# Retention and routed experts: decays as full products, tables built on the chip, loads ahead of row sends, and the first expert's weights by quarters

## The chip, the cores and the metric

The kernel runs on one core of one Trainium2 chip. The metric is the device time of one execution in microseconds (us); lower is better. Names of engines: PE is TensorE, DVE is VectorE, ACT is ScalarE, POOL is GpSimd, SP is SyncE, which here only issues DMA transfers. SPq and POOLq are the queues of instructions that SP and POOL issue.

## The reference

Retention over 4 batches, 8 heads, 768 steps and 64 values per head gives 3072 tokens of 512 values. These are routed greedily, by the highest logits first, to 8 experts with room for 384 tokens each, and every expert is two matrix products with a ReLU between them.

```python
gamma = 1.0 - 2.0 ** (-5.0 - np.arange(H, dtype=np.float32))
scale = 1.0 / np.sqrt(D)
for t in range(S):
    state = gamma[None, :, None, None] * state + np.einsum('bhd,bhe->bhde', k[:, :, t], v[:, :, t])
    y[:, :, t] = scale * np.einsum('bhd,bhde->bhe', q[:, :, t], state)
...
logits = x @ w_gate
order = np.argsort(-logits.flatten())
for idx in order:
    tok, e = (int(idx) // E, int(idx) % E)
    if assigned[tok] >= 0 or counts[e] >= cap:
        continue
    assigned[tok] = e
    counts[e] += 1
...
for e in range(E):
    mask = assigned == e
    h = np.maximum(x[mask] @ w1[e], 0.0)
    out[mask] = h @ w2[e]
```

## The kernel before

**Retention.** The 768 steps are cut into 6 chunks of 128, so there are 24 units (batch, chunk), chunk by chunk: unit 0 to 3 are chunk 0 of the four batches. Each unit comes in one load (`ld`) of 1 MB: keys and queries by columns, values and keys by rows (0.75 MB in the last chunk, which needs no state). There are 8 buffers for loads (DEEP), so the load of unit u + 8 needs the buffer of unit u. Units 0 to 3 are worked one at a time, the others two at a time (a group). Per unit PE does the scores (`scores`, 8 matmuls with 64 rows, recorded as 16), for chunks after the first the old state's part of the output (`outputs`), the mix of scores and values (`mix`) and the state's update (`states`). In between DVE multiplies the scores with the decay table `dm` into `am`, POOL scales keys (`ks`) and queries (`qs`), and ACT copies outputs (`ys`) and states (`T`).

**Start.** The decay table `dm` is made by `decays`: 8 matmuls of two tables with a single row each, times the triangle `upper`. PE runs matmuls on a tile of zeros (`warm`, function `busy`, counts in WARM) before the decays, before and after the scores of unit 0. The table `qtab` scales queries from chunk 1 on, `ktab` keys, `cst` and `thr` serve routing, `ident` is the unit matrix for transposes. All come by loads on SP, between the units' loads. SP's order is decided by the scheduler, PE's is that of the code, and within retention DVE's and ACT's also.

**Rows and routing.** Finished outputs become rows of tokens: 17 units by DVE transposes that SP sends to `xs` in memory (`block_rows`, `send_long`, `send_one`, 36 sends), seven by PE transposes (`early_rows`, `rows_out`), an ACT copy `xr` and a send. The logits go into a search over thresholds on DVE and PE (`search`): compare tokens with thresholds (`cmp`), count pairs by a matmul of `cmp` and the one-hot `oh` (`by_two`), and from the counts the threshold (`th`, `q`, `nmb` and others). Its result, the token list `idx`, lets POOL gather the expert's tokens (`xg`) and weights (`wraw`).

**Experts.** Each float32 operand is split into a high and a low part: `w1h` on ACT and `w1l` on DVE, `xh` and `xlo` the same after a turn of the gathered tokens on PE (`turn_x`, tile `pt`, two buffers). mm1 has for each of 8 blocks f twelve products of 128x384 (`ph`), mm2 24 products of 128x512 for each of 3 tiles of tokens (`py`). For expert 0 the first high products are done as thirds of 128 tokens as they arrive (`by_thirds`), after a fill of idle PE (HOT matmuls); mm1 then does the rest of these blocks. The search for the next expert (`side`) runs beside mm1 and mm2. A planner with estimated times (`clk`) sets the order of code; `side.held` stops the search from being stepped while an `xlo` is pending.

## Time and profile before

| | us |
|---|---|
| median of 3 runs (413.46 to 415.4) | 413.63 |
| profiled execution, own time | 416.51 |
| its span, first to last instruction | 414.7 |
| PE busy | 394.7 (95%) |
| DVE, ACT, POOL busy | 272.1, 157.5, 141.7 |
| mean granted clock of PE | 0.991 |

The own time of the profiled execution is 1.8 us more than its span, and 2.9 us more than the median of the runs. Of the span, retention takes about the first 91 us, routing and the start of the first expert's work the time to 117 us, and the eight experts the rest.

### The profile page before, as it was taken

Reading aid. Unit: us, or ns where it says so; the run is one execution under the profiler, and the core shown is the slowest. Engines: PE = TensorE matmul, PEld = TensorE weight load, DVE = VectorE, ACT = ScalarE, POOL = GpSimd, SP = SyncE. Lnnn points to the kernel's source line nnn. Section 1 sums busy time; section 2 is a strip of 40 time slices with the busy share of each in tenths; the row PEclk is TensorE's granted clock in tenths of the full one; section 3 lists DMA queues with packets and bytes.
Section 4 is the critical chain, followed back from the end, with each engine's and each line's share of the span. In section 5 each row is a group of like instructions: output and inputs, shape, how many; then the busy total and the mean of one; then the engine's idle time right before and its main releaser. Section 6 shows DMA issues by size and latency. Waiting matters only on the chain.

```text
span 414.7 us, 8494 instructions
## 1 busy us (share of the span) xinstructions
PE 394.7 (95%) x3464; PEld 343.8 (83%) x3465; DVE 272.1 (66%) x637; ACT 157.5 (38%) x287; POOL 141.7 (34%) x158
## 2 busy tenths in 40 slices
PE   8999988997899999998999999998999999999994
PEld 7888987986499779886887897897789889989983
DVE  1438768796989758766977795779488457246400
ACT  1342332423346056133525343543344347156210
POOL 2369873300520440074044251134125217120011
PEclk9999999998999999998999999999999999999999
DMA  7999997937673291339329447047325714901001
GB/s 239 415 417 420 398 307 255 268 83 235 194 286 106 60 320 77 103 109 338 112 55 322 145 140 305 25 149 258 129 66 173 293 51 119 387 28 51 2 27 57
DMA packets 23538, 77.99 MB, mean 188 GB/s; under 512 B 2626, under 2 KB 11970, under 8 KB 17092
## 3 DMA queue, kind: packets, MB, share of 16 engines
q0 software_dynamic: 8592, 46.14, 32.1%
q1 hardware_dynamic: 14900, 31.23, 21.1%
q8 instruction: 29, 0.48, 0.5%
q14 instruction: 17, 0.14, 0.1%
HBM read 64.78 MB, written 12.58 MB: 187 GB/s over the span
## 4 chain that ended last, share of the span: by engine, by line
PE 60%; issue 14%; DVE 11%; DMA 9%; POOL 2%; ACT 2%; SPq 0%; POOLq 0%; DVEq 0%
PE py L1038 23%; PE ph L1016 22%; DMA ld<-qkv 9%; PE yp L388 3%; PE sc L343 2%; PE pt L966 2%; PE psm L146 2%; DVE w2l L146 1%; POOL out L1046 1%; PE yp L373 1%; PE TP L407 1%; DVE cmp L146 1%; POOL wraw L914 1%; PE sc L473 1%; PE ph L995 1%
## 5 line engine op out<-in xcount | busy, mean ns | idle before, releaser
L1016 PE MATMUL ph<-xh,w1h 128*128 128x384 f32 x244 | 81.4, 348 | 2.5 <-ACT xh L971 1.5
L1016 PE MATMUL ph<-xh,w1l 128*128 128x384 f32 x256 | 81.7, 338 | 0.0
L1016 PE MATMUL ph<-xlo,w1h 128*128 128x384 f32 x256 | 81.3, 336 | 0.0
L1038 PE MATMUL py<-w2h,hh 128*128 128x512 f32 x192 | 78.1, 407 | 0.0
L1038 PE MATMUL py<-w2l,hh 128*128 128x512 f32 x192 | 75.2, 392 | 1.0 <-DVE w2l L146 1.0
L1038 PE MATMUL py<-w2h,hl 128*128 128x512 f32 x192 | 75.1, 391 | 0.0
L1046 POOL DMA_INDIRECT out<-yo,oix x24 | 26.1, 1086 | 104.4 <-ACT yo L1044 85.2
L1021 ACT ACTIVATE hh<-ph 128x384 fp32r<-128x384 f32 x64 | 31.5, 491 | 64.2 <-PE ph L1016 61.3
L146 DVE SCALAR_TENSOR_TENSOR hl<-ph,hh 128x384 fp32r<-128x384 f32 x64 | 34.6, 553 | 25.7 <-ACT hh L1021 25.3
L914 POOL DMA_INDIRECT wraw<-w,wix x31 | 33.9, 1093 | 47.4 <-DVE un L146 34.3
L1016 PEld LDWEIGHTS ph<-xh,w1h 128*128 128x128 f32 x244 | 45.9, 190 | 4.0 <-ACT xh L971 1.9
L146 DVE TENSOR_TENSOR w1l<-wraw,w1h 128x1024 fp32r<-128x1024 f32 (+1 forms) x36 | 39.3, 1102 | 14.4 <-ACT w1h L932 14.2
L1016 PEld LDWEIGHTS ph<-xh,w1l 128*128 128x128 f32 x256 | 48.2, 190 | 0.0
L953 POOL DMA_INDIRECT xg<-xs,idx x24 | 30.9, 1288 | 49.6 <-issue 33.5
L1016 PEld LDWEIGHTS ph<-xlo,w1h 128*128 128x128 f32 x256 | 47.8, 189 | 0.0
L346 DVE TENSOR_TENSOR am<-sc,dm 128x512 f32<-128x512 f32 x48 | 30.1, 683 | 25.0 <-PE sc L343 25.0
L1038 PEld LDWEIGHTS py<-w2l,hh 128*128 128x128 f32 x192 | 36.2, 188 | 8.2 <-DVE w2l L146 2.2
L1038 PEld LDWEIGHTS py<-w2h,hl 128*128 128x128 f32 x192 | 36.0, 188 | 7.7
L1038 PEld LDWEIGHTS py<-w2h,hh 128*128 128x128 f32 x192 | 36.1, 188 | 5.9
L1044 ACT ACTIVATE yo<-py 128x512 f32<-128x512 f32 x24 | 14.4, 599 | 67.3 <-PE py L1038 37.1
L146 DVE TENSOR_TENSOR w2l<-wraw,w2h 128x1024 fp32r<-128x1024 f32 x32 | 38.5, 1218 | 1.4 <-ACT w2h L932 1.4
L932 ACT ACTIVATE w1h<-wraw 128x1024 fp32r<-128x1024 f32 (+1 forms) x36 | 33.8, 957 | 7.3 <-DMA wraw<-w,wix 7.2
(169 smaller groups left out, 548.3 us busy)
## 6 DMA issues: line engine op xcount, KB each, us to landing
ld<-qkv SPq DMA_DIRECT2D x19, 1024.0 KB, 13.2
xs<-x SPq DMA_DIRECT2D x16, 192.0 KB, 5.2
ld<-qkv SPq DMA_DIRECT2D x4, 768.0 KB, 6.2
xs<-xr SPq DMA_DIRECT2D x7, 256.0 KB, 2.1
xs<-x SPq DMA_DIRECT2D x20, 64.0 KB, 1.8
ld<-qkv SPq DMA_DIRECT2D x2, 512.0 KB, 5.6
wraw<-w,wix POOLq DMA_INDIRECT x33, 7.3
xg<-xs,idx POOLq DMA_INDIRECT x24, 3.8
```

Source lines behind the costliest of these rows:

```text
L146: return f(o, *a, **k)
L343: nc.tensor.matmul(sc[s][:, pr, :], k_[r, w], q_[r, w], start=True, stop=True)
L346: nc.vector.tensor_tensor(am[:, s], sc[s], dm[:, s], op=OP.mult)
L388: nc.tensor.matmul(yp[o:o + 64, pr, :], values(u)[:, 2 * pr + s, :], st[u][0][:, s, pr, :], start=(not c and pr == 0), stop=(pr == HP - 1) ...
L914: nc.gpsimd.indirect_dma_start(out=t, out_offset=None, in_=w1v if nm == "w1" else w2v, in_offset=bass.IndirectOffsetOnAxis(ap=wix[:, hf:hf ...
L932: nc.scalar.activation(p[0], p[2], AF.Copy)
L953: nc.gpsimd.indirect_dma_start(out=t, out_offset=None, in_=xs, in_offset=bass.IndirectOffsetOnAxis(ap=found[n][0][:, j:j + 1], axis=0))
L1016: nc.tensor.matmul(ph, a[:, o:o + 128], x_[:, d], start=(k == 0 and not begun), stop=(k == len(prods) - 1), skip_group_check=begun)
L1021: nc.scalar.activation(hh[:, f], ph, AF.Relu)
L1038: nc.tensor.matmul(py, h_[:, f, t], a[:, o:o + DM], start=(k == 0), stop=(k == 23))
L1044: nc.scalar.activation(yo, py, AF.Copy)
L1046: sct = nc.gpsimd.indirect_dma_start(out=out, out_offset=bass.IndirectOffsetOnAxis(ap=oix[:, j:j + 1], axis=0), in_=yo, in_offset=None, bo ...
```

## The change

The decay table is made from products of 128 rows: the two single rows are copied into tiles that are zero elsewhere. The triangle `upper`, `ident`, the triangle `ub` and the counting row `iot` are built by POOL; `qtab` is made by one matmul of 2 rows and an ACT copy (`q_decay`); `cst` shrinks from 229 to 37 columns, and `thr` is loaded after the last unit. Unit 0 comes in one transfer in place of two. SP follows the order of the code, which places every send of rows behind the last load. Within a group, each unit's states follow its own mix. The last row transposes are spread differently (early_rows three in place of two, by one each). The second 512 KB quarter of w1 is fetched behind the three gathers of x, and its high and low parts are made after the thirds; the thirds cover blocks 0 and 1 in place of 0, 1 and 2. The search's steps are held for experts 0 and 1 while an `xlo` is pending, before only for expert 0. Numbers of warming and filling matmuls change with it.

```diff
-WARM = (10, 4, 6)
+WARM = (12, 6, 6)
...
 SEND = 10, 12
-EARLY = 2
-COLD = 2
-HOT = 22
-THIRDS = 3
+COLD = 4
+HOT = 18
+THIRDS = 2
 FILL = (4, 7)
...
     def consts_on_chip():
-        for t, name in ((ub, "tri"), (codet, "code"), (codeo, "code"), (tokc, "tokc")):
+        for t, name in ((codet, "code"), (codeo, "code"), (tokc, "tokc")):
             nc.scalar.activation(t, c_(name), AF.Copy)
 
     def constants():
         for t, x in [(onesb, 1.0), (un, 1.0)] + [(t, 0.0) for t in (zer512, Sc, Wq, bad, *sgs)]:
             nc.gpsimd.memset(t, x)
+        nc.gpsimd.affine_select(ub, onesb, pattern=[[1, 128]], compare_op=OP.is_gt, fill=0.0, base=0,
+                                channel_multiplier=-1)
+        nc.gpsimd.affine_select(ident, onesb, pattern=[[1, 128]], compare_op=OP.is_equal, fill=0.0, base=0,
+                                channel_multiplier=-1)
+        nc.gpsimd.iota(iot, pattern=[[1, 64]], base=0, channel_multiplier=0, allow_small_or_imprecise_dtypes=True)
 
...
     nc.vector.memset(warm, 0.0)
-    dec = [rw.tile([1, H, C], F32, name="am", bufs=4) for _ in range(2)]
+    dec = [rw.tile([128, 2, HP, C], F32, name="am", bufs=4) for _ in range(2)]
+    rowd = [rw.tile([1, 2, HP, C], F32, name="am", bufs=4) for _ in range(2)]
+    qsel = rc.tile([2, 128], F32, name="qsel")
+    qr = rw.tile([2, HP * C], F32, name="qs", bufs=4)
     up = rw.tile([128, HP, C], F32, name="qs", bufs=4)[:, 0]
+    nc.vector.memset(dec[0], 0.0)
+    nc.gpsimd.memset(dec[1], 0.0)
+    nc.gpsimd.memset(up, 1.0)
+    nc.gpsimd.affine_select(up, up, pattern=[[1, C]], compare_op=OP.is_ge, fill=0.0, base=0, channel_multiplier=-1)
 
...
             for i in range(2):
-                nc.sync.dma_start(dec[i], decay[:, i])
-            nc.sync.dma_start(up, upper)
-        ways = ((0, 2), (2, 4)) if u == 0 else ((0, 4),) if c < NC - 1 else ((0, 3),)
-        for w0, w1_ in ways:
-            nc.sync.dma_start(LD[u][:, w0:w1_], qkv[u, :, w0:w1_])
-            if u == 0 and w0 == 0:
-                nc.sync.dma_start(ktb, ktab)
+                nc.sync.dma_start(rowd[i], decay[:, i])
+        w1_ = 4 if c < NC - 1 else 3
+        nc.sync.dma_start(LD[u][:, 0:w1_], qkv[u, :, 0:w1_])
+        if u == 0:
+            nc.sync.dma_start(ktb, ktab)
+            nc.sync.dma_start(qsel, qrow[:, 0:128])
+            nc.sync.dma_start(qr, qrow[:, 128:])
         if u == B:
             nc.sync.dma_start(wgf, wg)
-            nc.sync.dma_start(ident, idm)
-        if u == B - 1:
-            nc.sync.dma_start(qtb, qtab)
-        if u == B + 1:
+        if u == B + 2:
             nc.sync.dma_start(cs, cst)
+        if u == nu - 1:
             nc.sync.dma_start(ti, thr)
 
     def decays():
 
         for s in range(2):
+            for i in range(2):
+                nc.vector.tensor_copy(dec[i][0:1, s], rowd[i][:, s])
+        for s in range(2):
             ps = bank()
             for pr in range(HP):
-                h = 2 * pr + s
-                nc.tensor.matmul(ps[:, pr, :], dec[0][:, h, :], dec[1][:, h, :], start=True, stop=True)
+                nc.tensor.matmul(ps[:, pr, :], dec[0][:, s, pr, :], dec[1][:, s, pr, :], start=True, stop=True)
             nc.vector.tensor_tensor(dm[:, s], ps, up[:, None, :].to_broadcast([128, HP, C]), op=OP.mult)
 
+    def q_decay():
+
+        ps = bank()
+        nc.tensor.matmul(ps.rearrange("p a b -> p (a b)"), qsel, qr, start=True, stop=True)
+        nc.scalar.activation(qtb, ps, AF.Copy)
+
     def bank():
...
     units = [(b, c) for c in range(NC) for b in range(B)]
+    nu = len(units)
+    ctx.enter_context(tc.manual_schedule(engines={nc.tensor.engine, nc.sync.engine}))
     for u in range(DEEP):
...
 
-    ctx.enter_context(tc.manual_schedule(engines={nc.tensor.engine}))
     wp = rp.tile([128, 512], F32, name="sc", bufs=4)
     busy(WARM[0], wp[:, 0:256])
     m0, a0, oh0, cmp0 = prep_tiles()
     parts, whole, ended, th0 = None, [], None, None
-    nu = len(units)
     groups = [[u] for u in range(B)] + [[u, u + 1] for u in range(B, nu, 2)]
...
             if not g:
+                q_decay()
                 busy(WARM[2], wp[:, 0:256])
...
                 guess()
-            mix(us)
-            states(us)
+            for u in us:
+                mix([u])
+                states([u])
             if g == len(groups) - 2:
...
             send_one(i)
-        early_rows(EARLY // 2)
+        early_rows(1)
         c = NC - 1
         gate(c)
-        early_rows(EARLY // 2)
+        early_rows(1)
         lt = rp.tile([128, 512], F32, name="sc", bufs=4)
         nc.tensor.transpose(lt[:, 0:128], gs[c % 2], ident)
         cols, Lc = slice(c, COLS, NC), lt[:, 0:128].rearrange("p (b x) -> p b x", b=B)[:, :, 0:E]
         f = best(Lc, cols, m0, oh0)
         reach(cols, B, m0, cmp0, th0)
         f()
+        early_rows(1)
         for b in range(B):
...
             raw["w1", 0, 0] = mp.tile([128, 2048], F32, name="wraw", bufs=5)
-            for k in range(2):
-                fetch_first(k, wix4)
+            firsts["w1"] = wix4
+            fetch_first(0, wix4)
         if not last:
...
         fetch_x(0, j)
+    fetch_first(1, firsts.pop("w1"))
     fetch_w("w1", 1, 0, found[0][1])
     for _ in range(4):
         side.step()
     fill(HOT)
     quarters = [parts_w("w1", 0, 0, 512 * q, 512) for q in range(4)]
-    for p in quarters[0:3]:
+    for p in quarters[0:2]:
         high_w(p)
     lows = []
     for j in range(KT):
         turn_x(0, j, lows)
         if not j:
             side.step()
-            high_w(quarters[3])
         else:
             by_thirds(j - 1, range(THIRDS))
-        low_w(quarters[j])
+        if j < KT - 1:
+            low_w(quarters[j])
         lows.pop(0)[1]()
     by_thirds(KT - 1, range(THIRDS))
-    low_w(quarters[3])
+    for p in quarters[2:4]:
+        high_w(p)
+        low_w(p)
     nc.gpsimd.tensor_copy(spacer, xt[0][0][0:1, HP - 1, CAP - 1:CAP].bitcast(F32))
...
     feed = Feed()
-    side.held = lambda: not feed.n and feed.xlows
+    side.held = lambda: feed.n < 2 and feed.xlows
     clk.pe = max(clk.pe, arrive["x", KT - 1, 0] + 2500)
```

SP, the loads of the start, before (`am` holds the decay rows and `qs` the triangle here, `ktb`, `qtb`, `wgf`, `cs`, `ti` are tables):

```order
L306 DMA am<-decay 1x1024 x2
L307 DMA qs<-upper 128x128
L310 DMA ld<-qkv 128x1024
L312 DMA ktb<-ktab 128x72
L310 DMA ld<-qkv 128x1024
L310 DMA ld<-qkv 128x2048 x3
L317 DMA qtb<-qtab 128x512
L310 DMA ld<-qkv 128x2048
L314 DMA wgf<-wg 128x256
L315 DMA ident<-idm 128x128
L310 DMA ld<-qkv 128x2048
L319 DMA cs<-cst 128x229
```

SP, the same place in the change (`qs` now holds the row from which `qtb` is made, `qsel` the two rows that select it):

```order
L317 DMA am<-decay 1x1024 x2
L319 DMA ld<-qkv 128x2048
L321 DMA ktb<-ktab 128x72
L322 DMA qsel<-qrow 2x128
L323 DMA qs<-qrow 2x512
L319 DMA ld<-qkv 128x2048 x4
L325 DMA wgf<-wg 128x256
L319 DMA ld<-qkv 128x2048 x2
L327 DMA cs<-cst 128x37
```

Between the first table and the load of unit 8 stand fewer and smaller tables. SP, the last loads and the first sends of rows, before:

```order
L310 DMA ld<-qkv 128x2048 x14
L450 DMA xs<-x_490 32x12x128
L310 DMA ld<-qkv 128x1536 x2
L450 DMA xs<-x_490 32x12x128 x3
L310 DMA ld<-qkv 128x1536 x2
L450 DMA xs<-x_492 32x12x128 x4
```

and in the change:

```order
L319 DMA ld<-qkv 128x2048 x13
L319 DMA ld<-qkv 128x1536 x4
L329 DMA ti<-thr 128x256
L467 DMA xs<-x_510 32x12x128 x4
L467 DMA xs<-x_512 32x12x128 x4
L467 DMA xs<-x_619 32x12x128 x4
```

One send stood before the load of unit 20 and three before that of unit 22; now all loads and `ti` stand ahead of them.

PE at the first expert, before: the turns of the second and third tile of x (`pt`, `py`), the thirds (128x128) and the beginning of mm1:

```order
L966 MATMUL pt<-ident,xg 128x128 x4
L995 MATMUL ph<-xh,w1h_1784 128x128 x12
L966 MATMUL py<-ident,xg 128x128 x4
L995 MATMUL ph<-xh,w1h_1784 128x128 x24
L1016 MATMUL ph<-xh,w1l_1785 128x384 x4
L1016 MATMUL ph<-xlo,w1h_1784 128x384 x4
L1016 MATMUL ph<-xh,w1l_1785 128x384 x3
```

and in the change:

```order
L986 MATMUL pt<-ident,xg 128x128 x4
L1015 MATMUL ph<-xh,w1h_1800 128x128 x8
L986 MATMUL py<-ident,xg 128x128 x4
L1015 MATMUL ph<-xh,w1h_1800 128x128 x16
L1036 MATMUL ph<-xh,w1l_1801 128x384 x4
L1036 MATMUL ph<-xlo,w1h_1800 128x384 x4
L1036 MATMUL ph<-xh,w1l_1801 128x384 x4
L1036 MATMUL ph<-xlo,w1h_1800 128x384 x4
```

Between the turns stand 8 thirds in place of 12, behind them 16 in place of 24, and the third block of mm1 is no longer begun.

DVE at the turn from expert 1 to expert 2, before: the search's steps (`sg`, `nmb`, `th`, `cmp`, `q`), the low parts of weights (`w1l`) and of x (`xlo`):

```order
L146 TENSOR_TENSOR w1l_2597<-wraw,w1h_2596 128x1024
L146 SCALAR_TENSOR_TENSOR sg_89<-psm,ng 64x8
L146 TENSOR_REDUCE nmb<-psm 128x1
L146 SCALAR_TENSOR_TENSOR th<-nmb,near,off 128x64
L146 TENSOR_TENSOR cmp<-m,th 128x768
L146 TENSOR_TENSOR w1l_2597<-wraw,w1h_2596 128x1024
L146 TENSOR_TENSOR cmp<-m,th 128x768
L146 SCALAR_TENSOR_TENSOR q<-nmb,near,qn 128x1
L146 TENSOR_TENSOR xlo<-pt,xh 128x4x128 x3
L146 TENSOR_TENSOR w1l_2704<-wraw,w1h_2703 128x1024
```

and in the change:

```order
L150 TENSOR_TENSOR w1l_2605<-wraw,w1h_2604 128x1024
L150 SCALAR_TENSOR_TENSOR sg_90<-psm,ng 64x8
L150 TENSOR_TENSOR w1l_2605<-wraw,w1h_2604 128x1024
L150 TENSOR_TENSOR xlo<-pt,xh 128x4x128 x2
L150 TENSOR_REDUCE nmb<-psm 128x1
L150 SCALAR_TENSOR_TENSOR th<-nmb,near,off 128x64
L150 TENSOR_TENSOR cmp<-m,th 128x768
L150 TENSOR_TENSOR xlo<-pt,xh 128x4x128
L150 TENSOR_TENSOR w1l_2709<-wraw,w1h_2708 128x1024
L150 SCALAR_TENSOR_TENSOR hl<-ph,hh 128x384
L150 TENSOR_TENSOR cmp<-m,th 128x768
L150 SCALAR_TENSOR_TENSOR q<-nmb,near,qn 128x1
```

The second `w1l` and two `xlo` now stand ahead of the search's `nmb`, `th` and `cmp`, the third `xlo` behind the first `cmp`.

## Rows read from the trace of the kernel before

**Rows 1.** Stretches of retention: PE, PEld, DVE, ACT, POOL busy; PEclk, DMA share, GB/s.

```profile
9.00:41.00 32.00, 29.77 (x545) 26.59 (x543) 17.29 (x32) 9.92 (x29) 21.06 (x19) 1.00 1.02 417
40.00:91.40 51.40, 48.90 (x1064) 44.21 (x1064) 40.72 (x94) 16.09 (x43) 25.48 (x22) 1.00 0.82 273
```

**Rows 2.** PE at the last wait for a load; PE's waits until 92.

```profile
40.02 1.16 PE L343 MATMUL sc<-ld 64*128 64x128 f32 x16 [0.92 <-DMA ld<-qkv]
PE sc L343 <- DMA ld<-qkv: 2.2, 3, 0.9
```

**Rows 3.** PE's timeline: start, duration, engine, line, operation, tiles, count, idle before.

```profile
3.31 3.78 PE L328 MATMUL sc<-am 1*128 1x128 f32 x16
7.99 2.08 PE L343 MATMUL sc<-ld 64*128 64x128 f32 x16
11.61 1.16 PE L343 MATMUL sc<-ld 64*128 64x128 f32 x16 [0.30 <-DMA ld<-qkv]
```

**Rows 4.** Timeline of PE and DVE at the search's start; stretch 95:100.

```profile
95.98 0.24 PE L146 MATMUL sc<-oh,cmp 128*128 128x16 bf16 x4 [0.84 <-DVE oh L146]
96.71 1.10 PE L418 MATMUL py<-ident,ys 128*128 128x128 f32 x4
100.20 0.45 PE L146 MATMUL psm<-oh,cmp 128*128 128x16 bf16 x12
97.45 1.83 DVE L146 TENSOR_TENSOR cmp<-m,th 128x768 bf16<-128x768 f32 x2
95.00:100.00 5.00, 3.70 (x23) 3.58 (x23) 3.73 (x13) 2.26 (x6) 0.00 (x0) 0.66 0.76 230
```

**Rows 5.** PE and DVE, turn from expert 1 to 2; stretch 192:195.

```profile
189.15 0.39 PE L1038 MATMUL py<-w2h,hl 128*128 128x512 f32 x1
190.64 0.63 PE L966 MATMUL pt<-ident,xg 128*128 128x128 f32 x4 [1.10 <-issue]
191.95 1.33 PE L1016 MATMUL ph<-xh,w1h 128*128 128x384 f32 x3 [0.69 <-ACT xh L971]
189.85 1.28 DVE L146 TENSOR_TENSOR xlo<-pt,xh 128x512 fp32r<-128x512 f32 x2
192.00:195.00 3.00, 3.00 (x9) 2.69 (x9) 1.85 (x2) 0.85 (x1) 0.00 (x0) 0.50 1.02 352
```

**Rows 6.** SP's queue: first unit load, last loads, sends of rows.

```profile
1.85 0.42 SPq L310 DMA_DIRECT2D ld<-qkv  x1
67.84 0.83 SPq L310 DMA_DIRECT2D ld<-qkv  x2
68.76 28.10 SPq L450 DMA_DIRECT2D xs<-x  x32
```

**Rows 7.** POOL and DVE at the start.

```profile
0.94 0.53 POOL L112 MEMSET zer<- 128x512 bf16 x1
9.16 1.04 POOL L353 TENSOR_TENSOR ld<-ld,ktb 128x512 f32<-128x512 f32 x1 [7.45 <-DMA ld<-qkv]
10.10 1.29 DVE L346 TENSOR_TENSOR am<-sc,dm 128x512 f32<-128x512 f32 x2 [2.28 <-PE sc L343]
```

**Rows 8.** PE, POOL and ACT at the first expert.

```profile
114.86 2.87 PE L995 MATMUL ph<-xh,w1h 128*128 128x128 f32 x24
120.54 0.85 PE L1016 MATMUL ph<-xh,w1l 128*128 128x384 f32 x4
121.93 0.33 PE L1016 MATMUL ph<-xh,w1h 128*128 128x384 f32 x1
107.28 0.95 POOL L953 DMA_INDIRECT xg<-xs,idx  x1 [0.93 <-DVE idx L146]
111.22 0.94 POOL L914 DMA_INDIRECT wraw<-w,wix  x1 [0.30 <-issue]
117.84 0.63 ACT L932 ACTIVATE w1h<-wraw 128x512 fp32r<-128x512 f32 x1 [2.03 <-DMA wraw<-w,wix]
```

**Rows 9.** PE at the turn from expert 0 to 1.

```profile
153.29 0.96 PE L1016 MATMUL ph<-xh,w1h 128*128 128x384 f32 x4 [0.79 <-ACT xh L971]
```

More of the change, by code (lines that the diff above doesn't have):

```diff
@@ L61, in tile_retention_moe @@
 @with_exitstack
-def tile_retention_moe(ctx: ExitStack, tc: tile.TileContext, qkv, wg, idm, w1, w2,
-                       decay, upper, qtab, ktab, thr, cst, out):
+def tile_retention_moe(ctx: ExitStack, tc: tile.TileContext, qkv, wg, w1, w2,
+                       decay, qrow, ktab, thr, cst, out):
     nc = tc.nc
@@ L82, in tile_retention_moe @@
     ub = sw.tile([128, 128], BF, name="ub")
-    iot = c_("iota")
+    iot = sw.tile([128, 64], F32, name="iot")
     bad = sw.tile([128, 1], F32, name="bad")
@@ L1253 @@
 import numpy as _np
-_PARTS = (("tri", 128), ("iota", 64), ("code", E), ("tokc", COLS), ("pcol", 1), ("wrow", 2), ("wrow4", 2),
+_PARTS = (("code", E), ("tokc", COLS), ("pcol", 1), ("wrow", 2), ("wrow4", 2),
 )
@@ L1268, in _tables @@
     gh = g.reshape(HP, 2)
-    upper = (i[None, :] >= i[:, None]) * 1.0
-    decay = _np.stack([g[:, None] ** (C // 2 - i)[None], g[:, None] ** (i - C // 2)[None] * sc])[None]
+    decay = _np.stack([g[:, None] ** (C // 2 - i)[None], g[:, None] ** (i - C // 2)[None] * sc])
+    decay = decay.reshape(1, 2, HP, 2, C).transpose(0, 1, 3, 2, 4)
     t = _np.arange(S).reshape(NC, C) - S // 2
-    qtab = _np.repeat(gh.T[:, :, None] ** (i - C // 2) * sc, 64, axis=0)
+    qrow = (gh.T[:, :, None] ** (i - C // 2) * sc).reshape(2, HP * C)
+    qrow = _np.concatenate([_np.repeat(_np.eye(2), 64, axis=1), qrow], axis=1)
     ktab = g[None, None, :] ** (-t.T[:, :, None])
@@ L1289, in _tables @@
     cst = {
-        "tri": (p[:, None] < p[None, :]) * 1.0,
-        "iota": _np.tile(p[None, :64] * 1.0, (128, 1)),
         "code": _np.tile(E - _np.arange(E)[None] * 1.0, (128, 1)),
@@ L1299, in _tables @@
     f = lambda a: _np.ascontiguousarray(a, dtype=_np.float32)
-    return f(decay), f(upper), f(qtab), f(ktab), _np.ascontiguousarray(thr), f(cst)
+    return f(decay), f(qrow), f(ktab), _np.ascontiguousarray(thr), f(cst)
 def kernel(q, k, v, moe_w_gate, moe_w1, moe_w2):
@@ L1311, in cols @@
         return a.reshape(B, HP, 2, NC, C, D).transpose(3, 0, 2, 5, 1, 4).reshape(NC * B, 128, DM)
-    decay, upper, qtab, ktab, thr, cst = _tables()
+    decay, qrow, ktab, thr, cst = _tables()
     wg = _np.zeros((128, 2, HP, 32), _np.float32)
@@ L1320 @@
     w2 = _np.ascontiguousarray(moe_w2.reshape(E, FT, 128, DM).transpose(0, 2, 1, 3)).reshape(E * 128, FT * DM)
-    arrays = {"qkv": qkv, "wg": wg, "idm": _np.eye(128, dtype=_np.float32), "w1": w1, "w2": w2,
-              "decay": decay, "upper": upper, "qtab": qtab, "ktab": ktab, "thr": thr, "cst": cst}
+    arrays = {"qkv": qkv, "wg": wg, "w1": w1, "w2": w2,
+              "decay": decay, "qrow": qrow, "ktab": ktab, "thr": thr, "cst": cst}
     nc = _bacc.Bacc("TRN2", target_bir_lowering=False, num_devices=1)
```

## The prediction, on record before the change ran

> **What bounds the kernel now.** I read the page first: TensorE (PE) is busy for 95% of the span, so a gain can only be time in which PE waits or runs at its lower clock level. The views by stretch, of the start, of the waits and of the hand-overs between stages then say where such time lies. [...]
>
> *The load stream.* From 9 to 41 us the DMA moves 417 GB/s and PE is idle for 2.2 us; from 40 to 91.4 us the rate is only 273 GB/s and PE is busy for 48.9 of 51.4 us [rows 1]. So the stream of unit loads bounds the first 40 us, and PE the rest of retention. The wait at which this changes is the last one for a load: scores of unit 11 begin at 40.02 after 0.92 us without their data, and three such waits make 2.2 us in all [rows 2].
>
> [...]
>
> *The search's start.* The count of pairs stands on PE behind 18 row transposes, from 96.71 to 100.20, in a stretch with a mean clock of 0.66 [rows 4]. What it also needs, `cmp` on DVE, ends at 97.45 + 1.83 = 99.28.
>
> *The turn from expert 1 to expert 2.* mm2's last matmul starts at 189.15, the third turn of x at 190.64 and mm1 only at 191.95; then nine matmuls fill 192 to 195 at clock 0.50 [rows 5]. The third turn needs the `pt` that the first `xlo` frees, and `xlo` starts at 189.85 on DVE [rows 5], after the search's `cmp`.
>
> **The change, part by part.**
>
> *A, start and stream.* Ahead of unit 11 in the queue, `upper` (64 KB), `qtab` (256), `ident` (64), 192 of the 229 columns of `cst` (96) and `thr` (128) are gone: 608 KB, or 0.62 MB, at 417 GB/s [rows 1] 1.49 us. The first unit load was issued at 1.85, after `upper` [rows 6]; without that one it goes some 0.4 us earlier. Together 1.9 us: the data of unit 11 let its scores begin at 38.1 instead of 40.02. Is PE there by then? From 11.61 to 40.02 are 28.4 us, less the two later waits (2.2 - 0.30 = 1.9): 26.5 us of work [rows 2, 3]. If scores of unit 1 begin at 11.6 as now, PE arrives at 38.1: the gain is 1.9. It is carried to the end of retention, since PE is nearly gapless there [rows 1]. Bounds: if the lower level lasts through scores of unit 0, `am` (1.29 at 10.10, [rows 7]), six instead of four warming matmuls and the new `qtb` product, unit 1 begins near 12.7 and 0.8 is left; if the start is shorter and the waits at units 1 and 5 shrink too, 2.6. I take 1.9.
>
> The full decay products replace one-row products that take 3.78 us, 16 records for 8 matmuls [rows 3]. I cost the new ones at the same: they are as wide, and at the lower level unit 0's eight matmuls of the same width, 16 records, take 2.08. Ahead of them DVE does a memset and four copies of 1x512, at most the 0.65 of each half of `am` (1.29 for two, [rows 7]): 3.2 us. All that lies before unit 0's landing: its second half cannot be long done at 7.99, when its scores begin now, and 1 MB at 417 GB/s is 2.5 us. On GpSimd 3 selects, an iota and three memsets come in: by the nearest row, a memset of 128x512 at 0.53 [rows 7], about 3.7 us after 1.7, done near 5.4. GpSimd's first real work, `ks` of unit 0, starts at 9.16 [rows 7], so nearly 4 us of cover; without it, every microsecond moves `ks`, and it costs nothing until the states of unit 0 (near 13.6) want it. Lower bound nothing, upper bound in the rivals. `qtb` is needed by unit 4 near 20 us, ten after its copy on ACT: nothing. The states behind each unit's mix free a load slot one mix earlier, in a stretch that PE bounds: nothing.
>
> [...] The row: PE busy from 1.07, yet 2.08 us for 16 matmuls at 7.99 [rows 3]. [...]
>
> *SP's order.* One `xs` send stood before the load of unit 20 and three before unit 22. The loads of units 22 and 23 are issued at 67.84, 32 sends take the next 28.1 us and end at 96.86 [rows 6]. Now all 36 follow the last load, and `thr`. Four more at 28.10/32 = 0.88 are 3.5 us of SP's queue, part of which was waiting for DVE's transposes. Behind them stand the last rows (`xr`), and for these the x gathers wait, which now start at 107.28 [rows 8]. I cost it at nothing, with 3.5 as the upper bound and a rival.
>
> *B, the search.* The row transposes ahead of the count fall from 18 to 14. They took 3.49 us, 0.194 each, so four are 0.78; the end of `cmp` at 99.28 caps the gain at about 0.85, and at twice the clock four would be half as long, 0.39: the lower bound. The four now stand before the pairs of the last chunk, where PE waits 0.84 for `oh` [rows 4], which covers 0.78. I take 0.6.
>
> *C, the first expert.* The thirds shrink from 36 to 24 of 128x128. 24 took 2.87 [rows 8], 0.12 each, so 12 fewer are 1.4. In return f = 2 does four more products: its eight start from 120.54 to 121.93, 0.174 each [rows 8], so four are 0.7. Net 0.7. But the second quarter of w1 is now issued behind three x gathers, where the 1 MB fetch of w1's other half was, at 111.22; that landed before 117.84, where its `w1h` starts [rows 8]. Less B, quarter 2 lands by some 117.2, its `w1h` takes 0.63, its `w1l` 0.68, and f = 2 begins at 120.54 - 1.4 - 0.6 = 118.5: just in time or 0.3 late. I take 0.4; bounds 0.7 and a loss of 1.0.
>
> *D, expert 1 to 2.* DVE now does `w1l` twice and two `xlo` before the search's `cmp`. `pt` is then free when mm2 ends, so the third turn starts at 189.4, ACT's `xh` at 190.2 behind its `yo`, and mm1 near 190.85 instead of 191.95: 1.1. [...] At the turn from expert 0 to 1 PE is idle for 0.79 before mm1, whose next four matmuls take 0.96 [rows 9], at the level of before: a turn that waits for ACT alone lets the clock stand. D is 1.1 to 2.5.
>
> *E.* At the turn from expert 2 to 3 the third turn now stands only three matmuls (0.7 us) before mm2's end. A turn with nothing behind it leaves PE idle for 0.79 [rows 9]; three matmuls at 0.23 cover 0.7 of that. The remaining 0.1 is the lower bound; with `yo` ahead of `xh` on ACT, as in D, it may be 0.6. I take a loss of 0.3. From expert 4 on the order is the same.
>
> *Sum.* 1.9 + 0.6 + 0.4 + 2.5 - 0.3 = 5.1 against the profiled execution's own 416.5, so 411.4. That execution is 2.9 above the median of 413.63, and the fallen clock after the turn may be a part of this that the others do not have; then the median loses 5.1 - 1.4 = 3.7 and comes to 409.9, otherwise 5.1, to 408.5. I take **409.3**, between the two.
>
> **The rivals.**
>
> 1. *The start stays slow and the fall stays* (0.13). A is 0.8, B 0.4, C nothing, D 1.1, E -0.3: 2.0, so 411.6. For it: the level did not rise in the first 11 us. Against it: the stream's gain needs no clock.
>
> 2. *The sends come late* (0.08). If all 3.5 us of the four sends reach the x gathers, the first of which could otherwise start 0.6 earlier by B, all but 0.2 of the 3.7 is gone: 413.4. As the train now also waits for DVE, I take half, 1.8: 411.1 to 412. For it: 28.1 us of issue stand just ahead of the last rows. Against it: from the last send at 96.86 to the first gather at 107.28 are ten microseconds, of which the last rows need only a part.
>
> 3. *GpSimd's setup is long* (0.07): slower. No select and no iota is in the trace, and a memset is the nearest row. `ks` of unit 0 is 1.04 long [rows 7] and wanted at 13.6, so setup may last until 12.5 for nothing. From there the start moves one for one: at 14.4 A is gone, at 16.8 all of the gain (409.3 to 413.6), and at 18.9 the kernel is at 415.7, which is 17.2 us for seven operations: 2.5 us each, instead of 0.5. For it: all of them are new. Against it: 4 us of cover, and states want less. [...]
>
> 4. *More than forecast* (0.12): the start at full clock, D whole in the median and the earlier x gathers (less w1 ahead of them) shorten C by another 1: 405.5 to 407.
>
> The forecast holds 0.60, between 407 and 411.5.
>
> **Range and chances.** 0.5% (2.1 us) is about what a measurement of this kernel can tell from no change. Faster, below 411.6: forecast and rival 4 whole and a little of 2, 0.74. Same, to 415.7: 1 and the rest of 2, 0.19. Slower: 0.07, from rival 3. The range, 405.5 to 413.2, leaves out rival 3, the end of rival 2 and what my bounds miss, together some 2 in 10.
>
> **What would show it.** A: the last wait for a load is at or before 38.3, and scores of unit 1 begin by 11.6 with 1.16 us; wrong, if GpSimd's first `ks` begins after 12. B: the count of pairs begins 3 us or less after the search's first sum. C: mm1 of the first expert begins about 2 us earlier than now, when the 24 thirds end at 117.7, and no wait for `w1h` before f = 2. D: no clock of 0.5 after the turn, and mm1 within 1.6 us of mm2's last matmul. Sends: the first x gather begins within half a microsecond after `idx`; if it begins later, rival 2.

## The result and the profile after

The changed kernel takes 410.64 us (median of 7 runs, 408.74 to 411.18), the kernel before in the same comparison 414.49 (413.46 to 415.86): a ratio of 0.9895, interval 0.987 to 0.992. The forecast was 409.3, range 405.5 to 413.2. The profiled execution takes 409.91, its span is 408.1. Medians here are of all executions; the ratios leave out the few that ran in a slower state.

The page's busy time by engine, and the one costly group that got dearer:

```profile
PE 388.8 (95%) x3459; PEld 338.4 (83%) x3459; DVE 274.4 (67%) x642; ACT 157.3 (39%) x287; POOL 144.5 (35%) x164
...
L1058 PE MATMUL py<-w2l,hh 128*128 128x512 f32 x192 | 75.3, 392 | 2.5 <-DVE w2l L150 2.5
```

PE's share is what it was. In the second line PE now waits 2.5 us in all for the low parts of w2; the same group waited 1.0 before. Nothing in the prediction speaks of that.

A total doesn't tell where 6.6 us of span went, so I cut both timelines at the same instructions on PE (and the search's `idx` on DVE). The third column is another execution of the order of before, from experiment 8 (warming counts alone changed):

| stretch, us | before | after | order of before, again | forecast |
|---|---|---|---|---|
| start to the search's first sum | 96.68 | 93.03 | 96.43 | -1.9 (A) |
| to `idx` | 10.14 | 9.06 | 9.15 | -0.6 (B) |
| to mm2 of expert 0 | 26.25 | 26.24 | 26.24 | -0.4 (C) |
| to mm1 of expert 1 | 20.22 | 22.02 | 20.18 | none |
| to mm2 of expert 2 | 59.12 | 54.89 | 57.71 | -2.5 (D) |
| to mm1 of expert 3 | 18.78 | 19.04 | 18.79 | +0.3 (E) |

The third column is needed: in two stretches the profiled execution of before was slower than the order of its instructions makes it. Against the third column the change gives 3.4 + 0.1 + 0 - 1.8 + 2.8 - 0.3 = 4.2; the rest of the span is 0.4 longer in the change (183.81 against 183.45), so 3.85 in all, and the medians differ by 3.85.

**The start.** PE's timeline and its waits, to set beside [rows 2, 3]:

```profile
3.88 2.67 PE L339 MATMUL sc<-am 128*128 128x128 f32 x16
...
7.14 1.16 PE L360 MATMUL sc<-ld 64*128 64x128 f32 x16
...
10.05 1.16 PE L360 MATMUL sc<-ld 64*128 64x128 f32 x16
...
33.13 4.89 PE L360 MATMUL sc<-ld 64*128 64x128 f32 x64
```

```profile
PE sc L360 <- DMA ld<-qkv: 0.7, 1, 0.7
```

Unit 0's scores take 1.16 us, not 2.08: PE is at its higher level before them. (The two levels are read from these durations, 2.08 and 1.16 us for the 16 records of a unit's scores. The granted clock reads 1.00 at both, in the kernel before from 7 to 9 us and from 11 to 12, so it is not shown that they are levels of the clock; see experiment 10.) Unit 1 starts 1.56 earlier. One wait for a load of 0.7 is left of three with 2.2, and none stands before unit 11, whose scores are the last 16 of the 64 that start at 33.13. The stretches of [rows 1, 4, 5], with the same columns:

```profile
9.00:41.00 32.00, 31.18 (x612) 28.12 (x613) 19.08 (x35) 10.74 (x30) 22.36 (x20) 1.00 1.02 420
40.00:91.40 51.40, 49.02 (x1052) 43.63 (x1049) 40.40 (x98) 16.96 (x48) 22.07 (x19) 1.00 0.84 262
95.00:100.00 5.00, 3.64 (x28) 1.50 (x24) 4.25 (x22) 2.45 (x6) 0.77 (x1) 1.00 0.86 315
192.00:195.00 3.00, 3.00 (x28) 2.84 (x28) 2.34 (x5) 2.13 (x5) 0.00 (x0) 1.00 0.78 303
```

The two falls of the clock, 0.66 and 0.50 before, are gone. GpSimd's setup and SP's queue, the places of rivals 3 and 2:

```profile
3.95 0.40 POOL L116 IOTA iot<- 128x64 f32 x1
6.67 1.04 POOL L370 TENSOR_TENSOR ld<-ld,ktb 128x512 f32<-128x512 f32 x1 [2.32 <-DMA ktb<-ktab]
...
65.48 27.73 SPq L467 DMA_DIRECT2D xs<-x  x36
...
102.55 0.95 POOL L973 DMA_INDIRECT xg<-xs,idx  x1 [2.17 <-DVE idx L150]
```

Setup is over at 4.35, and the first `ks` waits for its table, not for GpSimd. DVE's four copies take 2.18 us beside this setup (from 2.45), and 1.42 in experiment 12, where they begin at 5.27: some 0.8 us more, whose cause isn't shown and which the cover takes. The 36 sends take 27.73 us, less than 32 did before (28.10), and the first gather waits for `idx`: the sends aren't late.

**The turn from expert 1 to expert 2**, PE, beside [rows 5]:

```profile
186.10 0.39 PE L1058 MATMUL py<-w2h,hl 128*128 128x512 f32 x1
186.33 0.18 PE L150 MATMUL psm<-sg,onesb 128*128 128x8 bf16 x1
186.37 0.63 PE L986 MATMUL pt<-ident,xg 128*128 128x128 f32 x4
187.72 0.98 PE L1036 MATMUL ph<-xh,w1h 128*128 128x384 f32 x4 [0.71 <-ACT xh L991]
```

The third turn of x follows mm2's last matmul at once, and mm1 starts 1.62 us after that matmul's start, against 2.80 before.

**The loss**, mm2 of expert 0, PE and then DVE:

```profile
129.70 0.39 PE L1058 MATMUL py<-w2h,hh 128*128 128x512 f32 x1
131.19 0.50 PE L1058 MATMUL py<-w2l,hh 128*128 128x512 f32 x1 [1.10 <-DVE w2l L150]
...
135.45 0.50 PE L1058 MATMUL py<-w2l,hh 128*128 128x512 f32 x1 [0.65 <-DVE w2l L150]
```

```profile
122.22 1.21 DVE L150 TENSOR_TENSOR w2l<-wraw,w2h 128x1024 fp32r<-128x1024 f32 x1
123.36 0.15 DVE L150 TENSOR_REDUCE nmb<-psm 128x1 f32<-128x8 f32 x1
...
129.92 2.35 DVE L150 TENSOR_TENSOR w2l<-wraw,w2h 128x1024 fp32r<-128x1024 f32 x2
134.17 1.23 DVE L150 TENSOR_TENSOR w2l<-wraw,w2h 128x1024 fp32r<-128x1024 f32 x1 [1.90 <-ACT w2h L952]
```

One low part of w2 is made at 122.22, then the search for the next expert runs on DVE, and the next low part is begun only at 129.92, when mm2 has come to it: PE waits 1.10 us, and 0.65 once more for the fourth, whose high part comes late from ACT. In the order of before there is one such wait in this stretch, of 0.25 (experiment 8), so these waits are 1.5 of the 1.8 lost.

### The profile page after: what moved, and what is told of

It reads as the page before. It is cut to its first block, busy times and chain, and to the rows that moved or that the text cites. A ratio compares the mean times of both kernels' runs of the same rounds, so it can differ in the third digit from the quotient of the medians.

```text
span 408.1 us, 8488 instructions
## 1 busy us (share of the span) xinstructions
PE 388.8 (95%) x3459; PEld 338.4 (83%) x3459; DVE 274.4 (67%) x642; ACT 157.3 (39%) x287; POOL 144.5 (35%) x164
## 4 chain that ended last, share of the span: by engine, by line
PE 60%; issue 14%; DVE 11%; DMA 7%; POOL 3%; ACT 2%; POOLq 0%; SPq 0%; DVEq 0%; ACTq 0%
PE py L1058 24%; PE ph L1036 20%; DMA ld<-qkv 5%; PE sc L360 4%; PE yp L405 4%; DMA wraw<-w,wix 2%; PE yp L390 2%; PE pt L986 2%; PE psm L150 2%; PE TP L424 2%; DVE cmp L150 2%; DVE w2l L150 1%; POOL out L1066 1%; PE sc L490 1%; POOL wraw L934 1%
## 5 line engine op out<-in xcount | busy, mean ns | idle before, releaser
L934 POOL DMA_INDIRECT wraw<-w,wix x31 | 35.1, 1131 | 55.6 <-DVE un L150 42.8
L973 POOL DMA_INDIRECT xg<-xs,idx x24 | 29.8, 1241 | 54.2 <-issue 32.6
```

Of the source, the lines that this page charges most:

```text
L934: nc.gpsimd.indirect_dma_start(out=t, out_offset=None, in_=w1v if nm == "w1" else w2v, in_offset=bass.IndirectOffsetOnAxis(ap=wix[:, hf:hf ...
L973: nc.gpsimd.indirect_dma_start(out=t, out_offset=None, in_=xs, in_offset=bass.IndirectOffsetOnAxis(ap=found[n][0][:, j:j + 1], axis=0))
```

## The experiments

Twelve kernels ran. Ratios are to the kernel before in the same comparison; the change's own is 0.9895 [0.987, 0.992].

**1. One-row decay products in the changed kernel.**

```diff
-    dec = [rw.tile([128, 2, HP, C], F32, name="am", bufs=4) for _ in range(2)]
-    rowd = [rw.tile([1, 2, HP, C], F32, name="am", bufs=4) for _ in range(2)]
+    dec = rowd = [rw.tile([1, 2, HP, C], F32, name="am", bufs=4) for _ in range(2)]
```

> The changed kernel with one-row decay products again (no zeroed tiles, no copies); all else as changed. Theory (the full products bring the higher clock level early): scores of unit 0 take about 2.1 us again instead of 1.16, scores of unit 1 begin 0.8 to 1.6 us later than 10.05, the wait for a load at unit 5 shrinks, and the time rises by about 1 us. Rival (the clock follows PE's being busy, whatever its rows, and the shorter warm-up of before was at fault, or the start came earlier only through the loads): scores of unit 0 take 1.16 us as in the changed kernel and the time stays.

414.21 us, ratio 1.0007 [0.997, 1.0043]: the whole gain is gone. But its profile doesn't show why. PE's timeline:

```profile
3.80 2.35 PE L333 MATMUL sc<-am 1*128 1x128 f32 x16
...
6.84 1.16 PE L354 MATMUL sc<-ld 64*128 64x128 f32 x16
...
223.40 0.19 PE L150 MATMUL psm<-sg,onesb 128*128 128x8 bf16 x1 [2.63 <-DVE sg L150]
```

Unit 0's scores are fast here. What is lost in this execution is lost at the turn from expert 2 to 3, where ACT makes the search's `ng` 4 us late:

```profile
220.90 0.17 ACT L216 ACTIVATE ng<-psm 64x8 f32<-64x8 f32 x1 [8.33 <-PE py L1052]
```

So after this run I held that one-row products don't matter. Experiment 10 corrected that.

**2. The 608 KB of tables loaded again**, as dummies in their old places in SP's order.

```diff
+            table(0)
...
+        if u == B - 1:
+            table(1)
...
+            table(2)
+        if u == B + 1:
+            table(3)
+            table(4)
```

> The changed kernel with 608 KB of loads put back into SP's order where upper, qtab, ident, the larger cst and thr stood (they fill tiles that nothing reads). Theory (bytes ahead of unit 11 are what the stream gained): unit 11's query scaling on GpSimd begins 1.5 to 1.9 us later than 36.24, and the time rises by 1.5 to 2. Rival (a table costs more than its bytes, since each occupies one of the places of outstanding loads): 3 us or more later, and the time rises by 3.

413.25 us, ratio 0.9989 [0.9956, 1.0023]. PE's waits in its profile:

```profile
PE sc L372 <- DMA ld<-qkv: 2.6, 4, 1.0
```

The waits for loads are back at 2.6 us. Unit 11's query scaling begins at 38.93, 2.7 later than in the change (36.24): more than the theory's 1.5 to 1.9, less than the rival's 3. (What the rival's places rest on is in the trace of before: SP's issues of `cst` and `thr` wait 2.1 us each for a unit's load to land.) The search's first sum is at 94.04, only 1.0 after that of the change. The median loses 2.6; its ten executions run from 410.76, the profiled one, to 416.76, so one profile doesn't account for the rest.

**3. Unit 0 in two transfers again.**

```diff
+        ways = ((0, 2), (2, 4)) if u == 0 else ((0, 4),) if c < NC - 1 else ((0, 3),)
+        for w0, w1_ in ways:
+            nc.sync.dma_start(LD[u][:, w0:w1_], qkv[u, :, w0:w1_])
+            if u == 0 and w0 == 0:
+                nc.sync.dma_start(ktb, ktab)
```

> The changed kernel with unit 0 loaded in two transfers of 512 KB and ktab between them, as before. Theory (one transfer is worth nothing by itself): same time, unit 11 within 0.4 us of 36.24. Rival (the stream gets up to speed sooner with one transfer): unit 11 lands 0.5 to 1 us later and the time rises as much.

412.26 us, 0.9941 [0.9909, 0.9972]. Unit 11's query scaling begins at 37.24, 1.0 later than in the change, so the theory's 0.4 is missed. But the search's first sum is at 92.50, no later than in the change (93.03), so retention as a whole loses nothing by it; its turn from expert 2 to 3 is 1.5 longer, as in experiments 10 and 11 (below), which have nothing to do with unit 0.

**4. The search held for expert 0 only.**

```diff
-    side.held = lambda: feed.n < 2 and feed.xlows
+    side.held = lambda: not feed.n and feed.xlows
```

> The changed kernel with the search held for expert 0 alone, as before. Theory (this one line gives the turn from expert 1 to 2 its gain): the third turn starts at least 1 us after mm2's last matmul, mm1 of expert 2 begins 1.1 to 1.3 us later counted from mm1 of expert 1, with a stretch at clock 0.5 in some executions, and the time rises by 1.1 to 2.5. Rival (with the start's shift the planner puts the search elsewhere anyway): no change.

412.83 us, 0.9976 [0.9944, 1.0008]. PE:

```profile
187.61 0.63 PE L986 MATMUL pt<-ident,xg 128*128 128x128 f32 x4 [1.10 <-issue]
188.92 0.96 PE L1036 MATMUL ph<-xh,w1h 128*128 128x384 f32 x4 [0.69 <-ACT xh L991]
...
203.09 0.44 PE L1036 MATMUL ph<-xh,w1h 128*128 128x384 f32 x1 [0.67 <-DVE hl L150]
```

The third turn waits again as in [rows 5], and a wait for `hl` returns behind it. From mm1 of expert 1 to mm2 of expert 2 it is 57.67 us, as in the order of before (57.71), against 54.89. One line gives D's 2.8.

**5. The search also held while the first low part of w2 is pending for expert 0.**

```diff
-    side.held = lambda: feed.n < 2 and feed.xlows
+    side.held = lambda: feed.n < 2 and feed.xlows or feed.n == 0 and feed.low and feed.low[2] == ("w2", 0, 1024)
```

> The changed kernel with one more rule for the planner: while the low part of w2's second quarter of expert 0 is pending, the search takes no step. Theory (the changed order of weights puts that low part behind the search on VectorE, and this costs PE 1.25 us at the start of expert 0's mm2): that wait is gone, the later one of 0.8 us at w2's third quarter may stay, mm1 of expert 1 begins 1.2 to 2 us earlier counted from expert 0's mm1, and the time falls by 1 to 2 us against the changed kernel, to a ratio near 0.986. Rival (the search, held back, is late at the next turn instead): mm1 of expert 1 begins no earlier, ratio 0.9895 or above.

409.74 us, 0.9884 [0.9852, 0.9915]. PE:

```profile
131.50 0.50 PE L1058 MATMUL py<-w2l,hh 128*128 128x512 f32 x1 [0.81 <-DVE w2l L150]
```

Two waits of 1.10 and 0.65 have become one of 0.81, and mm2 of expert 0 to mm1 of expert 1 takes 21.22 in place of 22.02: 0.8, less than the 1.2 to 2 that I expected. The order on DVE is the cause of this part; the medians (0.9 apart) are within each other's intervals.

**6. Three tiny ACT copies at the start**, to shift where ACT's instructions fall.

```diff
+    def pad():
+        for _ in range(3):
+            nc.scalar.activation(spare, onesb[:, 0:1], AF.Copy)
```

> The changed kernel with three tiny copies more on ScalarE at the start, so that every later instruction of ScalarE stands three places further on in its program; no other work changes. Theory (in some executions ScalarE waits at the turn from expert 2 to 3 for its next instructions, which come by DMA among weights): the wait moves to a place where ScalarE has nothing urgent, no execution loses time there, and the median falls by up to 1 us while the slower executions become fewer. Rival (ScalarE waited there for data or a semaphore): the wait of 1.5 to 2.6 us at that turn appears as often as before and the time stays.

409.47 us, 0.989 [0.9854, 0.9927]: as the change. `ng` at the turn from expert 2 to 3 isn't late, but it wasn't in the change either; experiment 10 has the copies and is late. From 208 to 222 us the DMA view here has one packet of a queue that the profile names instruction (0.01 MB), beside 555 of the queue of weights, tokens and outputs (2.84 MB); no run shows ACT waiting for such a packet.

**7. Two early rows in place of three, COLD 2**: four more transposes ahead of the search's count, as before.

```diff
-COLD = 4
+COLD = 2
...
-        early_rows(1)
```

> The changed kernel with the third early row transpose taken away, so that 18 transposes stand ahead of the search's count again. Theory (fewer transposes ahead of the count is what the search gained): the count ends 0.35 to 0.8 us later counted from the search's first sum, with the clock at its lower level for part of it if PE's pauses lengthen, and the time rises by as much. Rival (with the clock up, 18 transposes at about 0.11 us are done before the comparison on VectorE ends, so the gain came from the clock alone): no difference beyond 0.2 us.

410.18 us, 0.9896 [0.9852, 0.9939]. From the search's first sum to its second 3.42 us, the same as in the change. The fewer transposes give nothing.

**8. The kernel before with the change's warming counts.**

```diff
-WARM = (10, 4, 6)
+WARM = (12, 6, 6)
```

> The kernel before with the changed kernel's warming counts (12, 6, 6) and nothing else. Theory (what PE is given to do at the start, not the decay products, decides when its clock rises): scores of unit 0 take 1.16 us instead of 2.08, scores of unit 1 still wait for their load until about 11.6, and the time falls by less than 0.5 us, as unit 1's load is what is waited for. Rival (the clock's rise is a matter of the single execution or of the loads): scores of unit 0 take about 2.1 us again, no change in time.

414.15 us, 1.0006 [0.9978, 1.0033]. The start is as slow as before; the windows of [rows 4, 5] aren't:

```profile
95.00:100.00 5.00, 3.22 (x39) 2.90 (x40) 3.98 (x15) 2.58 (x7) 0.00 (x0) 1.00 0.81 253
192.00:195.00 3.00, 3.00 (x28) 2.84 (x28) 1.58 (x4) 1.70 (x4) 0.00 (x0) 1.00 0.96 347
```

The order of instructions there is that of before, and the clock is 1.00. Both falls belonged to the one profiled execution.

**9. Experiments 5 and 6 together.** The edits are those two.

> The change with two edits that each won about one microsecond alone: the search held for expert 0 while the first low part of w2 is pending, and three tiny copies at ACT's start. If the two stalls that they remove are separate, their gains add: from the first mm1 of expert 0 to that of expert 1 37.6 us (38.85 in the change), no PE idle over 1 us at the turn from expert 2 to 3, span 405 to 406, median 408.3 to 409.3, ratio to before 0.984 to 0.988. Rival: the copies' gain is only the scatter of one run, or one stall is the other's shadow: 409.5 to 410.2, ratio 0.989.

411.18 us, 0.9911 [0.9874, 0.9948]: a miss. From mm2 of expert 0 to mm1 of expert 1 it takes 21.48, against 22.02 in the change and 21.22 in experiment 5, so that edit still does most of its work. In the profiled execution, one of the slowest of the seven (412.11), the loss is in retention; PE's timeline and the window behind:

```profile
56.20 0.42 PE L496 MATMUL sc<-ys,wgf 128*32 128x128 f32 x7
59.07 1.01 PE L496 MATMUL sc<-ys,wgf 128*32 128x128 f32 x25 [2.45 <-issue]
```

```profile
60.00:65.00 5.00, 5.00 (x70) 4.58 (x71) 2.68 (x5) 0.28 (x1) 0.26 (x1) 0.68 0.28 116
```

A wait of 2.45 us between two matmuls of the same product, for nothing that the profile shows, and then a mean clock of 0.68. The change has 0.87 at the same place and 1.04 a little later. Of the 3.2 us by which the search's first sum is later than in the change, 1.4 lie ahead of this wait, 0.5 are the longer waits, and 1.3 come behind. What the edits have to do with it is open.

**10. One-row decay products once more, with the copies of experiment 6**, which stand a little later in ACT's order here.

> One-row decay products again, with the three tiny ACT copies. Theory: one-row products cost nothing, and the 4 us that they seemed to cost are the late ACT step at the turn from expert 2 to 3, which the copies move: scores of unit 0 1.16 us, those of unit 1 before 10.2, no idle over 1 us at that turn, median 409.3 to 410.5. Rival 1: one-row products do hold the clock low, and the first run of them escaped by chance: scores of unit 0 2.08 us, those of unit 1 after 11, 411 to 412.5. Rival 2: the turn has another cause, and stays at 3 us idle: 413.5 to 414.5.

413.57 us, 0.9968 [0.9942, 0.9994]; that is 4.1 above experiment 6 (of another comparison), which differs by the products and the copies' place. PE's timeline, and a stretch of the start:

```profile
3.80 3.78 PE L339 MATMUL sc<-am 1*128 1x128 f32 x16
...
8.90 2.08 PE L360 MATMUL sc<-ld 64*128 64x128 f32 x16
...
14.30 2.08 PE L360 MATMUL sc<-ld 64*128 64x128 f32 x16
...
18.76 1.16 PE L360 MATMUL sc<-ld 64*128 64x128 f32 x16
```

```profile
12.00:20.00 8.00, 8.00 (x74) 6.02 (x74) 1.63 (x4) 1.19 (x2) 4.35 (x4) 1.00 1.02 424
```

Here the lower level stays to about 18 us (16 scores in 2.08 us at 14.30, in 1.16 at 18.76), the timeline shows no pause of PE from 1.12 on, and the search's first sum is at 95.73, 2.7 after that of the change. The granted clock of the stretch reads 1.00 all the same, so it doesn't tell the level here; the durations do. For the start, rival 1 of this experiment holds. Another 1.3 us is lost at the turn from expert 2 to 3, where `ng` is late once more, so the copies are no cure.

**11. w1 of the first expert as before**: both quarters fetched ahead of x, thirds over three blocks, HOT 22.

```diff
-HOT = 18
-THIRDS = 2
+HOT = 22
+THIRDS = 3
...
-            fetch_first(0, wix4)
+            for k in range(2):
+                fetch_first(k, wix4)
...
-    for p in quarters[2:4]:
-        high_w(p)
-        low_w(p)
+    low_w(quarters[3])
```

> The first expert's w1 as before: both quarters fetched ahead of x, thirds over three blocks, HOT 22. Theory: the change's w1 by quarters wins 0.7 us in thirds and loses about 2 by the order that the planner then gives DVE (w2's second low part behind the search): here both low parts of w2 stand ahead of the search again, mm1 of expert 0 starts as in the change but its third block 0.7 later, waits for w2l fall from 2.1 us to 0.4, mm1 of expert 1 starts 1 us earlier, 409.3 to 410. Rival: the low parts of w2 wait for the fetch, not for the order; then the loss stays and the thirds add 0.7: 411 to 411.8.

408.38 us (407.49 to 409.0), 0.9837 [0.9786, 0.9887]: the lowest median of all, though of four executions, and its interval overlaps that of the change. DVE, and then PE's waits:

```profile
120.91 2.36 DVE L150 TENSOR_TENSOR w2l<-wraw,w2h 128x1024 fp32r<-128x1024 f32 x2
123.18 0.16 DVE L150 TENSOR_REDUCE nmb<-psm 128x1 f32<-128x8 f32 x1
```

```profile
PE py L1058 <- DVE w2l L150: 1.0, 2, 0.7
```

Two low parts of w2 stand ahead of the search again, and the wait is 1.0 as in the kernel before. From `idx` to mm2 of expert 0 it takes 26.25 (26.24 in the change), from there to mm1 of expert 1 20.19 (22.02).

**12. The kernel before with the full decay products alone.**

```diff
+    nc.vector.memset(dec[0], 0.0)
+    nc.gpsimd.memset(dec[1], 0.0)
...
+            for i in range(2):
+                nc.vector.tensor_copy(dec[i][0:1, s::2], rowd[i][:, s::2])
```

> The kernel before with the full decay products alone. Theory 1 (one-row products hold the clock low in the kernel before): scores of unit 0 1.16 us, those of unit 1 at or before 11 with the wait for its load, median 412 to 413. Theory 2 (they do not; something else of the start, or the chance of one execution, sets when the clock rises): scores of unit 0 still 2.08 or a rise that comes without gain since the load stream sets the time of unit 11; 413.7 to 415, ratio within 0.4% of 1.

413.92 us, 0.9996 [0.9967, 1.0024]. PE:

```profile
6.08 3.78 PE L334 MATMUL sc<-am 128*128 128x128 f32 x16 [2.69 <-DVE am L329]
...
10.64 1.22 PE L349 MATMUL sc<-ld 64*128 64x128 f32 x16
...
12.55 0.71 PE L349 MATMUL sc<-ld 64*128 64x128 f32 x7
```

SP's order, here the scheduler's, puts the rows behind the triangle and half of unit 0, so DVE copies them at 5.27, PE pauses for 2.69, and all decays run at the lower level (3.78 us for the 16 records, 2.67 in the change). The scores of unit 0 are fast (1.22) and yet late; unit 1 starts at 12.55, against 11.61 [rows 3]. With their rows this late, full products give nothing; the kernel before with full products and early rows was not run.

## Why the prediction was right, and where it was off

**A, forecast 1.9, measured 3.4 to 3.65.** The mechanism held and the size was off, in two terms. One is "If scores of unit 1 begin at 11.6 as now": they begin at 10.05, since PE is at the higher level before unit 0's scores (1.16 us). I had seen the lower level in [rows 3] and put the fast start into rival 4. The other is the 1.9 of the stream: the tables alone move unit 11 by 2.7 (experiment 2). At the search's first sum, 2.7 of the 3.4 to 3.65 return in experiment 10 with one-row products, and 1.0 in experiment 2 with the tables. These are not clean shares, since PE's waits without a shown cause (last section) differ too: in retention they sum to 2.4 before (nearly all of PE's idle time behind 40 us in [rows 1]), 1.9 in the change, 0.8 in experiment 2 and none in experiment 10. Unit 0's single transfer gives nothing at the first sum (experiment 3).

On the level at the start: in the profiles, three of four starts with one-row products stay at the lower one to 10 us or longer (before, experiments 8 and 10, with 2.08 us for unit 0's scores), and all nine starts with full products in the change's order are at the higher one when unit 0's scores begin (1.16 us in the change and in experiments 2, 3, 4, 9 and 11). The fourth, experiment 1, rises while its one-row products run: 16 records took 2.35 us where the other three starts took 3.78. This speaks for the kind of product, but it doesn't decide alone: experiments 1 and 10 have the same instructions on PE up to there, and the level rises within the products in one and at about 18 us in the other. Whether the point of the rise varies from run to run of one kernel is not shown, since no kernel here has two profiles; that pair, which differs by three ACT copies, comes nearest.

**B, forecast 0.6, measured 0.1.** Against the kernel before's profile it looks like 1.08. But the order of before takes 9.15 in experiment 8 without the fallen clock, and experiment 7 shows that the four transposes give nothing: the count waits for `cmp` either way (0.56 us in the change, 0.33 in experiment 7). The step that failed is the price of 0.194 per transpose, which was read at a clock of 0.66; the lower bound of 0.39 fails too, since in experiment 7 the 18 transposes are done by 95.03, while `cmp` still runs.

**C, forecast 0.4, measured 0 up to mm2, then a loss of 1.8.** PE in the change:

```profile
111.50 0.92 PE L1036 MATMUL ph<-xh,w1l 128*128 128x384 f32 x4
...
119.43 0.31 PE L150 MATMUL psm<-oh,cmp 128*128 128x16 bf16 x6 [0.49 <-DVE cmp L150]
```

The first product of 128x384 stands 9.41 us after `idx`, against 10.75 before: 1.3 earlier (10.74 again in experiment 11, which undoes C). Four more products take 0.7 of that back, and a wait for the search's `cmp` in the middle of mm1 0.49, so that `idx` to mm2 is 26.24 against 26.25; no wait for `w1h` appears. Nine more profiles have this order: the three with that wait take 26.29 to 26.83, the six without it 25.60 to 26.07, so there C's first part comes out near the forecast. The loss behind is the step that the prediction left out: the second half of w1 is now split later, the planner gives DVE one low part of w2 fewer ahead of the search, and mm2 of expert 0 waits twice. Experiment 11 undoes C and the loss is gone, experiment 5 removes part of it by the order alone. The order of DVE behind the thirds was there to be read before the run; I looked at the turn from expert 1 to 2 only.

**D, forecast 1.1 to 2.5, measured 2.8** against an undisturbed order of before, by experiment 4's one line: 1.3 at the turn, as the first step said, and 1.5 behind it, which the prediction didn't see; a wait for `hl` is 0.67 of that, the rest isn't told apart. The 1.4 that makes D 2.5 in its sum, from a clock that no longer falls, no run shows as a gain of the change; in its place the runs show 1.41 between two executions of the order of before, 59.12 with the clock at 0.50 from 192 to 195 and 57.71 with 1.00, as "a part of this that the others do not have" allowed.

**E, forecast a loss of 0.3, measured 0.26** in the change, but 1.3 to 1.5 more in experiments 3, 10 and 11 and 4.1 more in experiment 1, always with ACT's `ng` late: it starts 2.4 to 3.9 us after the count that it reads, in the change 0.04. Why it is late in some is open: experiment 6 was meant to tell and did not.

**Rivals 2 and 3** fall by the rows on SP and GpSimd above. Rival 1 falls as well: the start is at the higher level (1.16 us for unit 0's scores), and the falls of the clock (0.66, 0.50) were those of one execution. Rival 4's conditions came, the fast start, D whole in the median and earlier data of x (the first turn 3.80 us after `idx`, 4.86 before), and yet not its time (405.5 to 407): C lost behind them.

The sum, 5.1 on the profiled execution, became 6.6; the median's 3.7 to 5.1 became 3.85. That the total came out is in part luck: against the median's sum of 3.7, which has D at 1.1, A and D brought 3.2 more, and B, C and the experts behind 3.1 less.

## What to carry to other kernels

Cut two executions at the same instructions and put a second execution of the old order beside them: two of the six differences here were in part the chance of one profile. Other profiles of the new order belong there too: C's first part is 0 in one and 0.6 in another. When a change moves work among an engine's instructions, read the new order up to the next hand-over, not only at the place that was moved: the 1.8 us were lost one stage later, on another engine. What pays in one order (products of full height) can give nothing in another (0.9996 in experiment 12), so an edit tried alone isn't disproved.

## What was not expected of the hardware

PE waits inside a product for nothing that its semaphores show, before the change (first two rows) and after it (last two, a row of the timeline and one of the waits):

```profile
59.65 0.84 PE L473 MATMUL sc<-ys,wgf 128*32 128x128 f32 x19 [1.05 <-issue]
67.39 0.85 PE L407 MATMUL TP<-ld 128*64 128x64 f32 x21 [1.37 <-issue]
...
56.10 0.92 PE L490 MATMUL sc<-ys,wgf 128*32 128x128 f32 x25 [0.87 <-issue]
...
PE yp L405 <- issue: 1.0, 1, 1.0
```

Thirteen of the fourteen profiles have the first of these waits (0.60 to 2.45 us; experiment 10 has none), and in all thirteen it stands behind the same number of matmuls on PE, 979, not at the same place of the work: the kernel before has six matmuls fewer ahead of this product and stops after 13 of its 32, the change after 7. The second wait, where there is one (0.21 to 1.37), stands 256 or 512 records of matmuls and weight loads after the first. Only the longest, the 2.45 of experiment 9, has a fall of the clock behind it (0.68 from 60 to 65 us). The DMA view of that one has one packet of a queue that the profile names instruction:

```profile
q1 hardware_dynamic: 149, 0.81, 97.3%
q8 instruction: 1, 0.02, 2.3%
```

The first row is the load stream, at 97% of the engines' time. The fixed count of 979 speaks against data as the cause. That the waits are for the supply of instructions is my guess and isn't shown: in the wait of 0.87 of the change no packet of an instruction queue lies, and no run separates that from other causes.
